# One more load buffer in the last batch, the chain to w_out's product cut into halves and parts, token logits kept in SBUF

## The chip, the cores and the metric

The kernel runs on one core of one Trainium2 chip. The metric is the time of one execution on the device in microseconds (us), as the median of several runs. Besides, one execution was profiled; it has a time and a span (first to last instruction) of its own.

## What is computed

Three layers follow each other, all in float32. Attention over 4 batches of 12 heads, 448 tokens and 64 columns gives `x` (1792 x 768), with a sigmoid in place of the softmax. Then

```
a = x @ w_a ; b = x @ w_b          # 768 -> 1536
x = (a * b) @ w_out                # 1536 -> 768
```

and last a layer of soft slots with 8 experts of 4 slots each:

```
logits = x @ phi                          # 1792 x 32
d = softmax of logits over all tokens     # per slot
slot_input = d.T @ x                      # 32 x 768
h = relu(slot_input[e] @ w1[e])           # 768 -> 1024, 8 experts
slot_out[e] = h @ w2[e]                   # 1024 -> 768
c = softmax of logits over the 32 slots   # per token
out = c @ slot_out                        # 1792 x 768
```

The experts' weights are read once: `w1` as 24 tiles of 128 x 2048 (1.05 MB each), `w2` as 32 tiles of 128 x 1536 (0.79 MB each), 50.3 MB in all.

## The kernel before, in words

The product with `w_out` is never formed for the tokens. The kernel keeps G = a * b (transposed, 12 chunks of 128 rows x 448 tokens per batch, five buffers `gT_all`), takes the logits as G times `wphi` = `w_out @ phi`, and sums d.T @ G over the batches into `acc`. Only that sum, 32 slots x 1536, is multiplied by `w_out` (line 773), which gives the slots' inputs.

A batch b of the part with w_a and w_b is the generator `ab` (line 476): 12 chunks, each of 18 matmuls for a and 18 for b (line 490), with `a` copied to `gT_all` by ACT (line 499) and multiplied by DVE (line 502). Into its gaps `fill_step` puts other work: `group` (line 445) adds four chunks to the logits `lps` (matmul line 453, add line 457) and turns them to token order (lines 467 to 469); `LG` (line 570) makes the running softmax over tokens (`logits`, line 522), turns logits and exponentials to token order (`tokens`, line 554), and adds to `acc` (`dg`, line 561). For batches 0 to 2 the logits in token order go from a tile `ltok` to a buffer `clog32` in HBM (line 579) and come back at the end (line 762). Attention of batch b + 1 runs beside batch b of `ab`. The weight halves of w_a and w_b are read for each batch again, 128 x 768 at a time (`load_w`, line 404), and split into a high and a low part by `split` (line 413: DVE or ACT, then POOL).

In the last batch, where attention is done, the room left is opened as load buffers ("slots") of 128 x 2048 for w_out (5 tiles, "wo"), w1 and w2. All of them are read in one order, `queue` (line 663). `pump` (line 669) takes the next tile of the queue and the next open slot and issues one load on SP; it is called 24 times in the last batch, and by `done` (line 698) whenever the products of a tile have freed its slot. Pool `e1` has 16 slots: 2 to 15 are open from the start of the last batch, slot 1 holds `lsd2` and slot 0 the raw weights `wr` first. `gkp` gives one slot. Pool `e2` lies in the room of the batch's x and split weights, which is free after the last a * b: its slots 1 to 4 are opened there (line 751), its slot 0 holds `gk_3` first and is opened after `last_LG` (line 758). That makes 22 slots.

`last_LG` (line 596) is the chain between the last a * b and w_out's product: logits of the last four chunks, sum over the four groups (`selF`, line 524), maximum, exponentials (line 541), exponentials to token order (line 558), `dg` (line 567) into `gp`, `acc` (line 614), its transposes (line 618), the copy to `GT` (line 619). Then come w_out's product (line 773), two steps that spread it to the experts (lines 776 to 783), w1's products (line 793, 24 tiles in groups of four), w2's (line 817) and the output.

The order on each engine is the order of the code; tiles wait for each other by semaphores which a layer below adds. SP issues its loads in order too, so a load that waits holds up those behind it.

Of the kernel before, what the change touches and what calls it, by code (L numbers as in the profile page):

```python
# [26 lines left out]
NE1, NE2 = 16, 5  # L27
# [6 lines left out]
def body(ctx, tc, q, k, v, w_a, w_b, w_out, phi, w1, w2, out):  # L34
# [55 lines left out]
    clog32 = drp.tile([T, C, B, NS], F32, name="clog32")  # L90
# [7 lines left out]
    clog = misc[:T, B * S + 256:B * S + 768].rearrange("p (c b s) -> p c b s", c=C, b=B)  # L98
# [300 lines left out]
    NCH = B * KF  # L399
    w_raw, w_sp = {}, {}  # L400
# [44 lines left out]
    def group(b, gi, evac=(act.copy, dve.tensor_copy) * 2):  # L445

        if (b, gi) != (B - 1, 2):
            for _ in range(GDEL):
                yield
# [8 lines left out]
        if (b, gi) == (B - 1, 2):  # L458
            gk = e2.tile([128, 2048], F32, tag="e20", name="gk_3")
        else:  # L460
            gk = gk_01[:, gi] if gi < 2 else gk_2
# [12 lines left out]
        gtok[b, gi] = gk  # L474

    def ab(b):
        for fc in range(KF):
# [7 lines left out]
            for i in range(2):  # L485
                wh, wl = ws[i]
                t = ps_tile("ab", [128, S], 2)
                for s, (w, xi) in enumerate(((wh, 0), (wh, 1), (wl, 0))):
# [5 lines left out]
                    if s == 2:  # L494
# [75 lines left out]
    def LG(b):  # L570
# [25 lines left out]
    def last_LG():  # L596

        run["ms"], run["lsd"] = 0, (lps, gT_all[3])
        lg, gr = logits(B - 1), group(B - 1, 2, (act.copy, dve.tensor_copy, act.copy, act.copy))
        next(gr)  # L600
        next(lg)
        next(lg)
        next(gr)
        next(lg)
        next(gr)
        dtok = stat.tile([T, C, NS], F32, tag="ltok", name="dtok", bufs=1)
        tokens(run["lsd"][1], dtok)
        for _ in gr:
            pass
        next(lg, None)  # L610
        gp = ms((128, FF // 4))
        for groups in ((0, 1), (2,)):
            dg(B - 1, dtok, gp, groups)
        dve.scalar_tensor_tensor(acc, acc, run["al"], gp, op0=ALU.mult, op1=ALU.add)
# [4 lines left out]
        act.copy(GT, gt)  # L619
        dve.tensor_scalar(rs, run["s"], 1e-9, None, op0=ALU.add)  # L620
        dve.reciprocal(out=rs, in_=rs)

# [43 lines left out]
    def open_slots(pl, names):  # L666
        slots.extend((pl, f"{pl.name}{i}") for i in names)

    def pump():

        if not queue or not slots:
            return
        what = queue.pop(0)
        pl, nm = slots.pop(0)
        t = pl.tile([128, 2048], F32, tag=nm, name=nm)
# [20 lines left out]
        ring[what] = t, pl, nm  # L696

    def done(what):
        slots.append(ring.pop(what)[1:])
        pump()  # L700
# [55 lines left out]
    run["banks"] = 2  # L756
    last_LG()
# [78 lines left out]
    for b in range(2 * B):  # L836
        pl, nm = slots.pop(0)
        o.append(pl.tile([128, 2048], F32, tag=nm, name="o")[:T, :2 * DM].rearrange(
# [37 lines left out]
```

## Time and profile before

| what | us |
|---|---|
| median of 3 runs | 737.91 |
| lowest, highest | 735.6, 739.79 |
| profiled execution, its own time | 734.16 |
| its span | 732.1 |
| PE busy in the span | 684.2 (93%) |

The 2.06 us between the profiled execution's time and its span lie around the first and last instruction. PE (TensorE) is busy most of the time, but not evenly: from some 200 us to the end of the last a * b at 609.8 us it is never idle, and after 640 us it waits for loads. The granted clock of PE is 1.00 of full speed nearly everywhere, and under it in some stretches after 660 us.

### The profile page before, as it was taken

To read this page: it belongs to the slowest core of one execution; us is meant where nothing else is said; L and a number is where in the kernel's file an instruction comes from. 1 tells how busy PE (TensorE), PEld (TensorE's weight loads), DVE (VectorE), ACT (ScalarE), POOL (GpSimd) and SP (SyncE) were. 2 spreads that over 40 slices of the span, in tenths; PEclk is the share of its full clock that TensorE was granted. 3 is DMA by queue.
4 is the path that set the end of the run, shared out by engine and by line. 5 is a ranking of instruction groups with operands and counts; after the bars stand their busy time and mean duration, and the time that the engine had idled before them with its cause. 6 is when DMAs were issued, how large, how long until landed. Compare 5 with 4: busy or idle time off the path is not lost.

```text
span 732.1 us, 10834 instructions
## 1 busy us (share of the span) xinstructions
PE 684.2 (93%) x4231; PEld 488.1 (67%) x4231; DVE 311.5 (43%) x452; ACT 271.9 (37%) x469; POOL 246.4 (34%) x151
## 2 busy tenths in 40 slices
PE   6999998999999999999999999999999998996682
PEld 4446776777777687787776887868889895441131
DVE  3567998899853323233333232313322232210012
ACT  4778778679643414233144141330201002110021
POOL 0106766666662233242431432324444542000000
PEclk9999999999999999999999999999999999999986
DMA  8858999899971432322423222310978937999958
GB/s 225 195 150 237 300 293 284 270 288 278 291 210 43 133 100 68 117 78 81 155 61 107 87 80 75 87 45 3 324 288 316 351 88 297 402 416 416 416 202 288
DMA packets 102930, 148.99 MB, mean 204 GB/s; under 512 B 51168, under 2 KB 76512, under 8 KB 99808
## 3 DMA queue, kind: packets, MB, share of 16 engines
q1 hardware_dynamic: 102880, 148.31, 61.8%
q8 instruction: 33, 0.54, 0.3%
q14 instruction: 17, 0.14, 0.1%
HBM read 128.46 MB, written 19.83 MB: 203 GB/s over the span
## 4 chain that ended last, share of the span: by engine, by line
PE 75%; DMA 13%; DVE 5%; ACT 3%; POOL 1%; issue 1%; SPq 0%; DVEq 0%; ACTq 0%; POOLq 0%
PE ab L490 44%; PE sc L191 9%; DMA e<-in_moe_w 7%; PE sc L177 7%; PE sc L793 3%; PE ms L145 3%; PE ms L467 2%; DMA wr_cv<-in_moe_w_a 2%; DVE gk L315 2%; PE ms L453 1%; PE ab L177 1%; PE ms L567 1%; DMA wr_all<-in_moe_w_b 1%; DMA out<-w 1%; DMA kn<-in_k 1%
## 5 line engine op out<-in xcount | busy, mean ns | idle before, releaser
L418 POOL TENSOR_TENSOR wl<-wr_all,wh 128x768 fp32r<-128x768 f32 x50 | 92.3, 1846 | 204.9 <-DVE wh L417 122.7
L490 PE MATMUL ab<-xh,wh 128*128 128x448 f32 x576 | 142.1, 377 | 1.4 <-ACT wh L417 1.4
L490 PE MATMUL ab<-xh,wl 128*128 128x448 f32 x576 | 141.8, 376 | 0.0
L490 PE MATMUL ab<-xl,wh 128*128 128x448 f32 x576 | 136.2, 371 | 0.0
L490 PEld LDWEIGHTS ab<-xh,wh 128*128 128x128 f32 x576 | 103.3, 188 | 20.9 <-issue 10.9
L490 PEld LDWEIGHTS ab<-xh,wl 128*128 128x128 f32 x576 | 104.1, 188 | 18.2 <-issue 8.6
L490 PEld LDWEIGHTS ab<-xl,wh 128*128 128x128 f32 x576 | 106.0, 188 | 15.4 <-issue 7.3
L181 ACT ACTIVATE a<-sc,nlog 112x448 f32<-112x448 f32 x168 | 93.5, 639 | 59.3 <-PE sc L177 59.1
L320 POOL TENSOR_TENSOR w<-gk,cy 128x768 int32<-128x768 int32 x36 | 66.2, 1838 | 99.7 <-DVE gk L315 69.5
L502 DVE TENSOR_TENSOR misc<-misc,ab 128x448 f32<-128x448 f32 x48 | 29.7, 618 | 125.8 <-PE ab L490 125.8
L499 ACT COPY misc<-ab 128x448 f32<-128x448 f32 x48 | 25.7, 536 | 153.2 <-PE ab L490 148.4
L191 PE MATMUL sc<-a,vn 112*64 112x448 f32 x384 | 76.1, 544 | 0.0
L418 POOL TENSOR_TENSOR wl<-wr,wh 128x768 fp32r<-128x768 f32 x22 | 40.5, 1839 | 53.7 <-DVE wh L417 45.7
L191 PEld LDWEIGHTS sc<-a,vn 112*64 112x64 f32 x384 | 26.0, 137 | 41.5 <-issue 38.7
L417 DVE CAST wh<-wr_all 128x768 fp32r<-128x768 f32 x50 | 35.2, 704 | 37.1 <-POOL wl L418 22.9
L817 PE MATMUL sc<-e,gk 128*32 128x384 f32 x240 | 36.4, 584 | 14.5 <-DMA e<-in_moe_w 14.2
L418 POOL TENSOR_TENSOR wl<-w,wh 128x768 fp32r<-128x768 f32 x24 | 44.9, 1869 | 3.1 <-ACT wh L417 3.1
L202 ACT ACTIVATE xh<-sc 128x448 fp32r<-128x448 f32 x24 | 13.1, 544 | 70.5 <-PE sc L191 70.5
L313 DVE TENSOR_SCALAR mf<-gk 128x768 f32<-128x768 f32 x36 | 34.1, 947 | 8.1 <-ACT gk L302 7.8
L203 DVE TENSOR_TENSOR xl<-sc,xh 128x448 fp32r<-128x448 f32 x24 | 15.0, 623 | 52.2 <-ACT xh L202 52.2
L817 PEld LDWEIGHTS sc<-e,gk 128*32 128x32 f32 x240 | 10.4, 126 | 39.7 <-DMA e<-in_moe_w 26.2
L177 PE MATMUL sc<-qh,kh 64*112 64x448 f32 x168 | 35.0, 412 | 0.6 <-ACT qh L138 0.6
(166 smaller groups left out, 764.2 us busy)
## 6 DMA issues: line engine op xcount, KB each, us to landing
e<-in_moe_w SPq DMA_DIRECT2D x23, 1024.0 KB, 7.9
e<-in_moe_w SPq DMA_DIRECT2D x27, 768.0 KB, 15.1
wr_all<-ab SPq DMA_DIRECT2D x50, 384.0 KB, 3.4
wr_cv<-in_moe_w_a SPq DMA_DIRECT2D x12, 768.0 KB, 7.2
wr_all<-in_moe_w_b SPq DMA_DIRECT2D x12, 768.0 KB, 6.7
wr_all<-in_moe_w_out SPq DMA_DIRECT2D x12, 768.0 KB, 7.2
ab<-w SPq DMA_DIRECT2D x24, 384.0 KB, 7.3
wr<-ab SPq DMA_DIRECT2D x22, 384.0 KB, 4.0
```

The costliest lines, as they stand in the source:

```text
L145: pe.transpose(t[:, c * T:(c + 1) * T], a[:, c].rearrange("p h d -> p (h d)"), ident[:T, :T])
L177: pe.matmul(sc[h], kx[r, cs], qx[r], start=(i == 0), stop=(i == 2))
L181: act.activation(a, sc[h], AF.Sigmoid, bias=nlog[:T], scale=1.0 / math.sqrt(D))
L191: pe.matmul(pv_t[g][64 * h:64 * h + 64], qkv_t["v", g][:, h, c, :], a_t.pop((g, h, c)), start=(c == 0), stop=(c == C - 1))
L313: dve.tensor_scalar(mf, m, LOW, HIGH, op0=ALU.max, op1=ALU.min)
L320: pool.tensor_tensor(thirds(w), m.bitcast(I32), thirds(cy_t.pop(x)), op=ALU.add)
L417: rnd(wh, t)
L418: pool.tensor_tensor(wl, t, wh.bitcast(F32), op=ALU.subtract)
L490: pe.matmul(t, w[:, kk * 128:(kk + 1) * 128], xt[b * NP + kk][xi], start=(s == 0 and kk == 0), stop=(s == 2 and kk == KD - 1))
L499: act.copy(gT_all[n % 5], t)
L502: dve.tensor_tensor(g, g, t, op=ALU.mult)
L817: pe.matmul(sps[h][32 * j:32 * j + 32], hT[:, 2 * x + i, 2 * j + g], ring[order2[n + j]][0][:, i, c0:c0 + w], start=(g == 0 and x == 0 and ...
```

## The change

Three things change.

- Slots. `e1` has 17 slots, of which 2 to 16 (15 instead of 14) are open from the start of the last batch; the last two are of 128 x 1536 and take only the tiles wo 3, wo 4 and w2. `e2` has 4 instead of 5. The sum is 22 as before. `pump` looks for a slot that the next tile of the queue fits in, small ones first, and does nothing if there is none; `done` calls it until it does nothing.
- Chain. The last a * b, the logits' matmul and add, the sum over groups and the maximum go by halves of 224 columns; `dg` and `acc` in two parts (groups 0 and 1, group 2); the copy to `GT` in two parts; all 16 transposes to token order stand ahead of those of the exponentials. The copy of the logits out of PSUM (`ls_3`) moves from behind the exponentials to the end.
- Token logits. `clog` is a tile in SBUF that `tokens` writes directly; three writes to HBM and one read back are gone.

```diff
-NE1, NE2 = 16, 5
+NE1, NE2 = 17, 4
...
-                            dve.tensor_tensor(g, g, t, op=ALU.mult)
+                            for cs in HALF if n == NCH - 1 else (slice(0, S),):
+                                dve.tensor_tensor(g[:, cs], g[:, cs], t[:, cs], op=ALU.mult)
...
-        ltok = stat.tile([T, C, NS], F32, tag="ltok", name="ltok", bufs=1)
-        tokens(run["lsd"][0], ltok)
-        sp.dma_start(out=clog32[:, :, b], in_=ltok)
+        tokens(run["lsd"][0], clog[:, :, b])
...
     def last_LG():
...
+        for cs in HALF:
+            for j in range(4):
+                pe.matmul(t[32 * j:32 * j + 32, cs], wphi[:, 8 + j], gT[b, 8 + j][:, cs], start=True, stop=True)
+            dve.tensor_tensor(lps[:, cs], lps[:, cs], t[:, cs], op=ALU.add)
+        lf = ms()
...
+        for cs in HALF:
+            pe.matmul(lf[:, cs], selF.rearrange("p j s -> p (j s)"), lps[:, cs], start=True, stop=True)
...
+            for i in range(4):
+                pe.transpose(tps[c][:, i * 128:(i + 1) * 128], gT[b, 8 + i][:, c * T:(c + 1) * T], ident)
...
+        dve.tensor_reduce(mx, lf[:, HALF[0]], axis=AX.X, op=ALU.max)
+        dve.tensor_tensor(m1, run["m"], mx, op=ALU.max)
+        dve.tensor_reduce(mn, lf[:, HALF[1]], axis=AX.X, op=ALU.max)
+        dve.tensor_tensor(m1, m1, mn, op=ALU.max)
...
+        act.activation(d, lf, AF.Exp, bias=nm, accum_out=sm)
...
+        tokens(d, dtok)
+        act.copy(gk[:, 2], tps[2])
+        act.copy(gk[:, 3], tps[3])
...
+        dg(b, dtok, gp, (0, 1))
+        parts = (slice(0, 256), slice(256, 384))
+        dve.scalar_tensor_tensor(acc[:, parts[0]], acc[:, parts[0]], al, gp[:, parts[0]], op0=ALU.mult, op1=ALU.add)
+        dg(b, dtok, gp, (2,))
+        dve.scalar_tensor_tensor(acc[:, parts[1]], acc[:, parts[1]], al, gp[:, parts[1]], op0=ALU.mult, op1=ALU.add)
         gt = ms((128, FF // 4))
         for gi in range(3):
             cs = slice(gi * 128, (gi + 1) * 128)
             pe.transpose(gt[:, cs], acc[:, cs], ident)
-        act.copy(GT, gt)
+        act.copy(GT[:, parts[0]], gt[:, parts[0]])
+        act.copy(GT[:, parts[1]], gt[:, parts[1]])
...
+        act.copy(ls_3, lf)
...
+            small = pl.name == "e1" and i >= NE1 - 2
+            slots.append((pl, f"{pl.name}{i}", 1536 if small else 2048))
...
+        need = 1536 if queue and (queue[0][0] == "w2" or queue[0][0] == "wo" and queue[0][1] >= 3) else 2048
+        fit = [s for s in slots if s[2] >= need]
+        if not queue or not fit:
+            return False
         what = queue.pop(0)
-        pl, nm = slots.pop(0)
-        t = pl.tile([128, 2048], F32, tag=nm, name=nm)
+        slot = min(fit, key=lambda s: s[2] > need)
...
     def done(what):
-        slots.append(ring.pop(what)[1:])
-        pump()
+        slots.append(ring.pop(what)[1])
+        while pump():
+            pass
...
-    tokens(run["lsd"][0], clog[:, :, B - 1])
+    tokens(ls_3, clog[:, :, B - 1])
     experts_consts()
-    sp.dma_start(out=clog[:, :, :B - 1], in_=clog32[:, :, :B - 1])
```

What it does to the order shows at three places. In the rows, "waits X" names the semaphore of the engine or DMA queue waited for (PE_49, DVE_49, Activation_49, Pool_49, DMAHW0_49 to DMAHW7_49), x4 counts equal instructions in a row.

First, PE at the start of the chain, behind the last matmul of line 490. Before (`wphi` logits into tile ms, `selF` sum, transposes, exponentials to token order at line 558):

```order
L453 MATMUL ms<-misc,wphi 32x448 [waits PE_49]
L453 MATMUL ms<-misc,wphi 32x448 x2
L453 MATMUL ms<-misc,wphi 32x448 [waits DVE_49]
L524 MATMUL ms<-misc,selF 128x448 [waits DVE_49]
L467 MATMUL sc<-ident,misc 112x128 x8
L558 MATMUL sc<-ident,misc 112x32 [waits Activation_49]
L558 MATMUL sc<-ident,misc 112x32 x3
L467 MATMUL sc<-ident,misc 112x128 [waits PE_49]
```

Now (the lines are those of the changed kernel; 599 answers to 453, 606 to 524, 612 to 467, 555 to 558):

```order
L599 MATMUL ms<-misc,wphi 32x224 [waits PE_49]
L599 MATMUL ms<-misc,wphi 32x224 x2
L599 MATMUL ms<-misc,wphi 32x224 [waits DVE_49] x2
L599 MATMUL ms<-misc,wphi 32x224 x3
L606 MATMUL ms<-misc,selF 128x224 [waits PE_49]
L606 MATMUL ms<-misc,selF 128x224 [waits DVE_49]
L612 MATMUL sc<-ident,misc 112x128 x12
L612 MATMUL sc<-ident,misc 112x128 [waits PE_49]
L612 MATMUL sc<-ident,misc 112x128 x3
L555 MATMUL ab<-ident,misc 112x32 [waits Activation_49]
```

Two of the eight wphi matmuls wait for DVE: the fourth of the first half, for the first half of a * b, and the first of the second half; by its count that one waits for DVE's add of the first half. All 16 transposes now stand ahead of line 555.

Second, PE at the end of the chain, from the transposes of `acc` to w_out's product. Before (line 558 here turns the logits of the last batch to token order):

```order
L618 MATMUL ms<-ident,acc 128x128 [waits DVE_49]
L618 MATMUL ms<-ident,acc 128x128 x2
L558 MATMUL ms<-ident,misc 112x32 x4
L773 MATMUL sc<-e_4989,misc 32x512 [waits DMAHW7_49,Activation_49]
L773 MATMUL sc<-e_4989,misc 32x512 x3
```

Now (638 answers to 618, 806 to 773):

```order
L564 MATMUL ab<-gk_5777,dtok 32x128 [waits DVE_49]
L564 MATMUL ab<-gk_5777,dtok 32x128 x7
L638 MATMUL ms<-ident,acc 128x128 [waits PE_49]
L638 MATMUL ms<-ident,acc 128x128
L638 MATMUL ms<-ident,acc 128x128 [waits DVE_49]
L555 MATMUL ms<-ident,misc 112x32 [waits PE_49,Activation_49]
L555 MATMUL ms<-ident,misc 112x32 x3
L806 MATMUL sc<-e_4985,misc 32x512 [waits DMAHW5_49]
L806 MATMUL sc<-e_4985,misc 32x512 x3
```

The second part of `dg` (line 564 on gk_3) waits for DVE, which before it did not: by its count, for the add of the first part to `acc`. Line 555 waits for ACT, by its count for the copy of the logits at line 643, which stands behind both copies to `GT` on ACT; w_out's product stands behind it.

Third, SP's loads from the last a * b on. Before:

```order
L695 DMA e21_5752<-in_moe2_w1 128x2048 [waits PE_49]
L695 DMA e22_5754<-in_moe2_w1 128x2048 [waits DMAHW6_49]
L695 DMA e23_5756<-in_moe2_w1 128x2048
L695 DMA e24_5758<-in_moe2_w1 128x2048
L695 DMA e20_5856<-in_moe2_w1 128x2048 [waits DVE_49,PE_49,Activation_49]
L762 DMA misc_97<-clog32_104 112x4x96 [waits PE_49]
L695 DMA e12_5884<-in_moe2_w1 128x2048 [waits PE_49]
L695 DMA e13_5890<-in_moe2_w1 128x2048 [waits DMAHW4_49,PE_49]
L695 DMA e14_5896<-in_moe2_w1 128x2048 [waits DMAHW5_49,PE_49]
L695 DMA e15_5904<-in_moe2_w1 128x2048 [waits DMAHW6_49,PE_49]
L695 DMA e16_5912<-in_moe2_w1 128x2048 [waits DMAHW7_49,PE_49]
L695 DMA e17_5946<-in_moe2_w1 128x2048 [waits DMAHW0_49,PE_49]
```

Now:

```order
L726 DMA e21_5749<-in_moe2_w1 128x2048 [waits DMAHW3_49,PE_49]
L726 DMA e22_5751<-in_moe2_w1 128x2048
L726 DMA e23_5753<-in_moe2_w1 128x2048 [waits DMAHW5_49]
L726 DMA e20_5862<-in_moe2_w1 128x2048 [waits DVE_49,PE_49,Activation_49]
L726 DMA e12_5889<-in_moe2_w1 128x2048 [waits PE_49]
L726 DMA e13_5895<-in_moe2_w1 128x2048 [waits PE_49]
L726 DMA e14_5901<-in_moe2_w1 128x2048 [waits PE_49]
L726 DMA e15_5947<-in_moe2_w1 128x2048 [waits DMAHW2_49,PE_49]
...
L726 DMA e18_5953<-in_moe2_w1 128x2048 [waits DMAHW5_49,PE_49]
L726 DMA e115_5955<-in_moe2_w2 128x1536 [waits DMAHW6_49]
L726 DMA e116_5957<-in_moe2_w2 128x1536 [waits DMAHW7_49]
```

Before, w_out's product released five loads (e12 to e16) and w1's first group the next ones (from e17). Now it releases three (e12 to e14); e15 to e18 wait for w1's first group, and the two small slots e115 and e116, which w_out's product frees too, take the first tiles of w2 only behind them (the rows of e16 and e17, like that of e15, are left out).

## Rows read from the trace of the kernel before

**Rows 1.** The page, slices: what the DMA engines moved in 40 equal slices of 18.3 us.

```profile
GB/s 225 195 150 237 300 293 284 270 288 278 291 210 43 133 100 68 117 78 81 155 61 107 87 80 75 87 45 3 324 288 316 351 88 297 402 416 416 416 202 288
```

**Rows 2.** The chain that ended last, from 560 us on: start, length, what.

```profile
611.60 0.63 DVE misc L457
...
612.28 1.02 PE ms L524 x2
...
616.57 2.78 PE ab L567 x64
...
619.38 0.61 DVE acc L614
...
620.63 0.49 ACT misc L619
...
621.16 4.08 PE sc L773 x48
...
629.11 10.44 PE sc L793 x96
...
652.88 15.06 DMA e<-in_moe_w
...
706.07 1.48 PE sc L817 x10
```

**Rows 3.** SP's timeline in short windows from 605 us on: start, length, loads issued.

```profile
605.60 0.33 SPq L695 DMA_DIRECT2D e<-in_moe_w  x1
...
609.87 2.06 SPq L695 DMA_DIRECT2D e<-in_moe_w  x4
...
619.40 0.33 SPq L695 DMA_DIRECT2D e<-in_moe_w  x1
...
622.29 0.34 SPq L695 DMA_DIRECT2D e<-in_moe_w  x1
...
632.69 1.28 SPq L695 DMA_DIRECT2D e<-in_moe_w  x3
```

**Rows 4.** Line 695, window 605 to 606: the load issued at 605.60, issue to landing.

```profile
DMA to landing us min/median/max: 4.9/4.9/4.9
```

**Rows 5.** Windows: length, busy times (count), PE clock, DMA share, GB/s last.

```profile
540.00:580.00 40.00, 40.00 (x210) 35.58 (x212) 11.04 (x17) 4.28 (x8) 17.59 (x10) 1.00 0.90 332
...
609.90:612.00 2.10, 1.66 (x8) 0.16 (x5) 1.02 (x2) 0.00 (x0) 0.00 (x0) 1.00 0.51 105
...
621.00:628.00 7.00, 6.15 (x57) 3.48 (x57) 1.04 (x2) 1.17 (x3) 0.00 (x0) 1.00 0.99 345
628.00:640.00 12.00, 12.00 (x105) 4.22 (x104) 3.78 (x7) 1.22 (x2) 0.00 (x0) 1.00 1.02 419
633.20:707.00 73.80, 58.26 (x431) 19.75 (x424) 2.08 (x3) 2.30 (x5) 0.00 (x0) 0.91 0.98 398
```

**Rows 6.** Timeline of 605 to 632 us: start, length, engine, instruction.

```profile
609.95 0.62 DVE L502 TENSOR_TENSOR misc<-misc,ab 128x448 f32<-128x448 f32 x1 [6.35 <-PE ab L490]
...
613.13 1.04 PE L467 MATMUL sc<-ident,misc 128*112 128x128 f32 x8
...
613.34 0.62 DVE L527 TENSOR_REDUCE mx<-ms 128x1 f32<-128x448 f32 x1 [1.11 <-PE ms L524]
...
613.99 0.16 DVE L531 TENSOR_TENSOR mn<-mn,mx 128x1 f32<-128x1 f32 x1
...
614.38 0.63 ACT L541 ACTIVATE misc<-ms,nm 128x448 f32<-128x448 f32 x1
...
615.59 0.29 DVE L559 COPY dtok<-sc 112x128 f32<-112x128 f32 x1 [0.58 <-PE sc L558]
```

**Rows 7.** Groups by form on PE, 605 to 640 us: count, busy us, mean ns, idle before.

```profile
L567 PE MATMUL ab<-gk,dtok 112*32 112x256 f32 x32 | 1.9, 382 | 0.0
...
L567 PE MATMUL ab<-gk,dtok 112*32 112x128 f32 x32 | 1.1, 273 | 0.0
```

**Rows 8.** Groups by form on ACT, 600 to 732 us: count, busy us, mean ns.

```profile
L469 ACT COPY gk<-sc 112x512 f32<-112x512 f32 x2 | 1.2, 585 | 7.7 <-PE sc L467 7.7
```

More of the change, by code (lines that the diff above doesn't have):

```diff
@@ L89, in body @@
     out32 = drp.tile([128, KF, DM], F32, name="out32")
-    clog32 = drp.tile([T, C, B, NS], F32, name="clog32")
     idj = ident.rearrange("p (j s) -> p j s", j=4)
@@ L97, in body @@
     SI = small[:, 1536:2304]
-    clog = misc[:T, B * S + 256:B * S + 768].rearrange("p (c b s) -> p c b s", c=C, b=B)
+    clog = const.tile([T, C, B, NS], F32, name="clog")
     selE = small[:, 2304:2560].rearrange("p (j g m) -> p j g m", j=4, g=2)
@@ L399, in body @@
     NCH = B * KF
+    HALF = (slice(0, S // 2), slice(S // 2, S))
     w_raw, w_sp = {}, {}
@@ L445, in group @@
     def group(b, gi, evac=(act.copy, dve.tensor_copy) * 2):
-        if (b, gi) != (B - 1, 2):
-            for _ in range(GDEL):
-                yield
+        for _ in range(GDEL):
+            yield
         t = ms()
@@ L457, in group @@
             dve.tensor_tensor(lps, lps, t, op=ALU.add)
[L458 to L461, printed above, removed]
+        gk = gk_01[:, gi] if gi < 2 else gk_2
         gk = gk[:T].rearrange("p (c n) -> p c n", c=C)
@@ L596, in last_LG @@
     def last_LG():
[L598 to L610, printed above, removed]
-        gp = ms((128, FF // 4))
-        for groups in ((0, 1), (2,)):
-            dg(B - 1, dtok, gp, groups)
@@ L614, in last_LG @@
-        dve.scalar_tensor_tensor(acc, acc, run["al"], gp, op0=ALU.mult, op1=ALU.add)
+        b = B - 1
+        run["ms"] = 0
+        d = gT_all[3]
+        t = ms()
+        for cs in HALF:
[3 more added lines that the diff above has]
+        lf = ms()
+        mx, nm, mn, dm, sm, al, sn = (stat.tile([128, 1], F32, tag=x, name=x)
+                                      for x in ("mx", "nm", "mn", "dm", "sm", "al", "sn"))
@@ new lines, in last_LG @@
+        m1 = stat.tile([128, 1], F32, tag="m1", name="m1")
+        for cs in HALF:
+            pe.matmul(lf[:, cs], selF.rearrange("p j s -> p (j s)"), lps[:, cs], start=True, stop=True)
+        gk = e2.tile([128, 2048], F32, tag="e20", name="gk_3")[:T].rearrange("p (c n) -> p c n", c=C)
+        tps = []
+        for c in range(C):
+            tps.append(ms((T, 512)))
+            for i in range(4):
+                pe.transpose(tps[c][:, i * 128:(i + 1) * 128], gT[b, 8 + i][:, c * T:(c + 1) * T], ident)
@@ new lines, in last_LG @@
+        gtok[b, 2] = gk
+        dve.tensor_reduce(mx, lf[:, HALF[0]], axis=AX.X, op=ALU.max)
+        dve.tensor_tensor(m1, run["m"], mx, op=ALU.max)
+        dve.tensor_reduce(mn, lf[:, HALF[1]], axis=AX.X, op=ALU.max)
+        dve.tensor_tensor(m1, m1, mn, op=ALU.max)
+        dve.tensor_scalar(nm, m1, -1.0, None, op0=ALU.mult)
+        dve.tensor_tensor(dm, run["m"], m1, op=ALU.subtract)
+        act.copy(gk[:, 0], tps[0])
+        act.activation(d, lf, AF.Exp, bias=nm, accum_out=sm)
+        act.activation(al, dm, AF.Exp)
@@ new lines, in last_LG @@
+        dve.tensor_copy(gk[:, 1], tps[1])
+        dtok = stat.tile([T, C, NS], F32, tag="dtok", name="dtok", bufs=1)
+        tokens(d, dtok)
+        act.copy(gk[:, 2], tps[2])
+        act.copy(gk[:, 3], tps[3])
+        dve.scalar_tensor_tensor(sn, run["s"], al, sm, op0=ALU.mult, op1=ALU.add)
+        gp = ms((128, FF // 4))
+        dg(b, dtok, gp, (0, 1))
+        parts = (slice(0, 256), slice(256, 384))
+        dve.scalar_tensor_tensor(acc[:, parts[0]], acc[:, parts[0]], al, gp[:, parts[0]], op0=ALU.mult, op1=ALU.add)
@@ L618, in last_LG @@
             pe.transpose(gt[:, cs], acc[:, cs], ident)
-        act.copy(GT, gt)
-        dve.tensor_scalar(rs, run["s"], 1e-9, None, op0=ALU.add)
+        act.copy(GT[:, parts[0]], gt[:, parts[0]])
+        act.copy(GT[:, parts[1]], gt[:, parts[1]])
+        dve.tensor_scalar(rs, sn, 1e-9, None, op0=ALU.add)
         dve.reciprocal(out=rs, in_=rs)
+        act.copy(ls_3, lf)
     def combine_weights():
@@ L666, in open_slots, with slot_tile @@
     def open_slots(pl, names):
-        slots.extend((pl, f"{pl.name}{i}") for i in names)
+        for i in names:
+            small = pl.name == "e1" and i >= NE1 - 2
+            slots.append((pl, f"{pl.name}{i}", 1536 if small else 2048))
+    def slot_tile(s, name=None):
+        pl, nm, n = s
+        return pl.tile([128, n], F32, tag=nm, name=name or nm)
     def pump():
-        if not queue or not slots:
-            return
+        need = 1536 if queue and (queue[0][0] == "w2" or queue[0][0] == "wo" and queue[0][1] >= 3) else 2048
+        fit = [s for s in slots if s[2] >= need]
+        if not queue or not fit:
+            return False
         what = queue.pop(0)
-        pl, nm = slots.pop(0)
-        t = pl.tile([128, 2048], F32, tag=nm, name=nm)
+        slot = min(fit, key=lambda s: s[2] > need)
+        slots.remove(slot)
+        t = slot_tile(slot)
         if what[0] == "wo":
@@ L756, in body @@
     run["banks"] = 2
+    ls_3 = lps
     last_LG()
@@ L836, in body @@
     for b in range(2 * B):
-        pl, nm = slots.pop(0)
-        o.append(pl.tile([128, 2048], F32, tag=nm, name="o")[:T, :2 * DM].rearrange(
+        o.append(slot_tile(slots.pop(0), "o")[:T, :2 * DM].rearrange(
             "p (c n) -> p c n", c=2))
```

3 lines of the change are left out of this document (2 added, 1 removed).

## The prediction, made before the changed kernel was run

> **What bounds the kernel now.** I read the slices first, then the chain of waits for the end, SP's issues in that stretch, and last the load rate in windows. PE is never idle from 540 to 580 us [rows 5], and so up to the last a * b. The loads are idle at two places and full at the end: the rate falls to 88 GB/s in the slice 586 to 604 us and is 402 to 416 GB/s from 622 to 695 us [rows 1]. So the slots are full before the batch ends, and everything behind it is paced by loads. The chain says the same: from 652.88 us on its long pieces are loads, until PE's last w2 products at 706.07 us [rows 2]. From there to the end of the span (26 us) the change touches nothing. The end therefore moves by as much as the last load of w2 moves, and that depends on two things: how many bytes are still to be moved when the slots open, and whether SP has a load to issue at all times.
>
> **Bytes.** By the last a * b, 17 loads are issued before (5 of w_out, 12 of w1); the 17th goes at 605.60 us, four more at 609.87, one at 619.40 when `dg` has used gk_3, then five from 622.29 on as w_out's product frees its slots, and the next at 632.69 behind w1's first group [rows 3]. With the change 18 are issued by the last a * b, then three, one, three, and nothing until w1's first group: the two small slots fit w2 only, and the queue's head is w1. The 18th falls into the idle stretch, where it costs nothing. One load less is 1,049 KB, the read back of the logits another 172 KB; at 419 GB/s [rows 5] these are 2.9 us. The rate is 345 GB/s from 621 to 628 us against 419 behind [rows 5], while the 384-byte pieces of that read are under way; were all of this dip the read's, its going would give 7 x (419 - 345) = 518 KB, 1.2 us in all with its own bytes, so that the whole gain is at most some 3.7 us. That counts only while the loads never run dry.
>
> **The chain to w_out's product**, before from 609.95 us to 621.16 us. By DVE's 0.62 us for 448 columns and 0.16 for one [rows 6], 224 columns cost 0.39.
> - To the maximum's start. Before: product 0.62, logits 1.03 (end of 502 to 611.60), add 0.63, sum 1.11 (612.23 to 613.34) [rows 2, 6]. Now: 0.39; then the halves' matmuls. w1's matmuls, four side by side and two instructions each, take 10.44 x 8 / 96 = 0.87 us for 512 columns [rows 2], so 448 columns stream for 0.76 and half of them save 0.38: 0.65; add 0.39; the second half's logits only then, 0.65 and 0.15 for its four weight loads (my estimate); add 0.39; sum 0.73. That is 3.35 against 3.39: nothing won, since the second half waits for the first half's add.
> - Maximum to exponentials: 613.34 to 614.38, 1.04 us [rows 6]. The two halves of the reduction both wait for the whole sum, by the order of the matmuls and of DVE: one more start of 0.16 and one more small step, 1.30 in all, +0.26.
> - Exponentials to `dg`: before, dtok is ready at 615.88 [rows 6], but eight transposes stand ahead of `dg`, which starts at 616.57 [rows 2]. Now all 16 stand ahead of the exponentials' transposes, and at 1.04 us for eight [rows 6] they are through by then: -0.65.
> - `dg` to the transposes' end: 616.57 to 620.63 before [rows 2]. Now 1.9 us [rows 7], 0.05, the first add to acc 0.48 (0.61 less 128 columns at 1.05 ns), 0.05, 1.1 [rows 7], 0.05, the second add 0.34, one transpose 0.37 (estimate, of the 0.64 for three): 4.34, +0.28, as the second part waits for the first add.
> - Copy to w_out: 620.63 to 621.16, 0.53 [rows 2]. Now ACT copies 256 and 128 columns and then 448 of the logits, at 0.59 for 512 [rows 8] and 0.49 for 384 [rows 2] some 0.37, 0.28 and 0.53 less 0.16 of overlap; PE's transposes of the logits wait for the third and w_out stands behind them, 0.3 more: 1.35, +0.8.
>
> Sum: -0.04 + 0.26 - 0.65 + 0.28 + 0.8 = +0.65; w_out starts at 621.8 instead of 621.16.
>
> That the second half waits is in the order shown above; no row of the trace before has DVE at a PSUM tile that PE is writing. The Trainium skill ("PSUM — Partial Sum Buffer", section "PSUM bank collisions raise a hardware error") says that two engines must not touch one bank and quadrant at once, disjoint columns included, so software has to keep them apart. By that rule the sum stands; without it the first rival's would.
>
> **The queue.** The four tiles of w1's first group come free together, 632.69 - 621.16 = 11.53 us after w_out starts [rows 2, 3]. From an issue into an idle queue to the full rate it takes 1.6 us: 609.87 to 612.00 brought 105 GB/s x 2.1 us = 220 KB, as much as 0.5 us at full rate [rows 3, 5]. As upper end I take the lone load's 4.9 us to landing [rows 4] less 2.5 of transfer, 2.4. So the loads flow again at 621.8 + 11.53 + 1.6 = 634.95 us. What is left then is 4 of w1 and 32 of w2, 29.36 MB. Before, just that much was left at 633.2 us: 398 GB/s x 73.8 us = 29.37 MB [rows 5]. So the change ends **1.7 us later**. The other way round: with the change the queue is empty from 618.9 to 621.3 (three loads instead of four), from 623.8 to 624.5, and from 632 to 634.95 us, 6 us; against the gain of 3.7 that is some +2, which agrees. With 2.4 for the restart it is +2.5.
>
> The Trainium skill ("SBUF — State Buffer", section "The DMA setup-cost knee (why "@ 1 MiB" ≠ asymptote)") gives about 2 us as the fixed part of every transfer. With it for the 1.6 the sum would be +2.1, the same case; the lone load's 4.9 us are above its 2 + 1,049 KB / 436 GB/s = 4.4.
>
> What else moves costs nothing: the three writes of token logits leave SP's queue in stretches where PE is never idle; `tokens` writes the same 128 columns (0.29 us [rows 6]). DVE's reduction over 16 x 32 logits no longer waits for a load; PE is busy with w1 then.
>
> **The forecast** is 734.16 + 1.7 = 735.9 us against the profiled execution. The median of the runs is 737.91, 3.75 above that execution, so 739.6 us on its scale: +0.24%, which a measurement of this kernel can't tell from no change (it can tell some 0.5%, 3.7 us).
>
> **Rivals.**
> - *The halves overlap after all*, the add of one beside the matmul of the other. Then the exponentials start 1.3 us earlier than in my sum, but wait for the 16 transposes (2.1 us); `dg` starts at 615.1, runs in one piece of 2.8, and w_out starts at 619.7 even with the logits' copy ahead: 619.7 + 13.13 - 633.2 = -0.4, 737.5 us. Against it: the waits in the order. Chance 0.12.
> - *The loads never run dry*, because SP issues w1's rest earlier. Then the full 3.7 us come in: 734.2 us. It decides by e15's issue: it would have to come by 630.4 us, and it waits for w1's first group at 633.3. Chance 0.05.
> - *The extra load delays the weight halves of a and b*, which share its queue between 582 and 605 us. If one half lands later than PE needs it, PE stops for up to one load's 2.5 us, and w_out starts that much later: +4.2, 742.1 us, slower by 0.57%. For it: the load stands ahead of a weight half on SP. Against it: at 332 GB/s from 540 to 580 us, such pairs ran one after the other and PE was busy 40.00 of 40 us [rows 5]. It decides once a weight half is late by more than its lead over PE, which no row shows. Chance 0.11.
>
> My forecast has 0.72. Faster by over 0.5%: the second rival's 0.05 and a little scatter, 0.06. Slower by over 0.5%: most of the third rival, and the upper end of my sum with scatter, 0.13. Within: 0.81. The range runs from 736.5 (between the first two rivals) to 742.2 us (the third).
>
> **What would show it.** Right: the loads' rate near 0 for 2 to 3 us around 619 to 621 and again around 632 to 635; w_out's first product at 621.5 to 622; SP issuing three loads, then none for some 9 us; `dg` with a gap of 0.5 us between its parts; the last w2 products 1 to 3 us later than 706. Wrong: a load rate above 400 throughout 612 to 640, or w_out at 620 or earlier, or PE idle before 609.8 us.

## The result, and the profile after

| | before | with the change |
|---|---|---|
| median, us (20 runs each) | 736.32 | 739.34 |
| lowest, highest | 731.69, 740.16 | 736.67, 747.49 |
| profiled execution, its own time | 734.16 | 740.74 |
| its span | 732.1 | 738.7 |
| ratio of the times | 1 | 1.0054, interval 1.0032 to 1.0075 |

The change costs 0.54%, some 4.0 us (by the 95% interval 2.4 to 5.5). The medians lie 3.0 us apart and the means 3.9 (736.3 and 740.2), as a few executions of the changed kernel are long. The forecast was 739.6 us and +1.7 us. The sign came out, and the time lies in the range, but the change cost about twice what the sum says (1.8 times by the medians, 2.4 times by the ratio). The likeliest case, "no change that can be told", is just missed by the ratio: its bound is 0.5%, "slower by over 0.5%" had a chance of 0.13, and the interval reaches to both sides of that bound.

Two profiled executions can't be subtracted as they stand. The last a * b begins at 609.95 us before and at 612.78 after, though the two programs do nearly the same up to there (the changed one issues one load more and writes no token logits to HBM). So I count everything **from the start of DVE's last a * b product on** ("behind the last a * b"), and took three profiles of the kernel before and four of the changed one. How that reads in the changed kernel's own profile: first the chain, in the timeline of DVE and PE (start, length, engine, instruction, then the idle time before it and what ended it).

```profile
612.78 0.69 DVE L499 TENSOR_TENSOR misc<-misc,ab 128x224 f32<-128x224 f32 x2 [6.35 <-PE ab L486]
...
614.27 0.59 PE L599 MATMUL ms<-misc,wphi 128*32 128x224 f32 x8 [0.48 <-DVE misc L600]
...
618.14 0.40 PE L555 MATMUL ab<-ident,misc 32*112 32x32 f32 x4 [0.37 <-ACT misc L621]
...
618.92 1.93 PE L564 MATMUL ab<-gk,dtok 112*32 112x256 f32 x32 [0.38 <-DVE dtok L556]
621.46 1.08 PE L564 MATMUL ab<-gk,dtok 112*32 112x128 f32 x32 [0.60 <-DVE acc L632]
...
624.41 0.41 PE L555 MATMUL ms<-ident,misc 32*112 32x32 f32 x4 [1.07 <-ACT misc L643]
624.74 5.76 PE L806 MATMUL sc<-e,misc 128*32 128x512 f32 x48
```

Three waits are new, in the places that the forecast names: the second half's matmuls wait 0.48 us for DVE's add of the first half, the second part of `dg` 0.60 us for the first add to `acc`, and the logits' transposes 1.07 us for ACT's copy (line 643). w_out's product starts 12.03 us behind the last a * b; before it was 11.21 [rows 2, 6]. One thing was not expected: w_out's product takes 5.76 us instead of 4.08 [rows 2]. (The chain below and the table further down give 5.69 for it and a start of 624.81: they leave out its first 0.07 us, beside the last transposes.) The windows over it (length, busy times, PE's granted clock, DMA share, GB/s last) say why:

```profile
622.00:624.00 2.00, 1.24 (x23) 0.61 (x15) 0.57 (x3) 0.62 (x3) 0.66 (x1) 1.00 0.40 61
624.00:626.00 2.00, 1.59 (x12) 0.69 (x16) 0.29 (x1) 0.35 (x1) 0.00 (x0) 0.69 0.81 311
626.00:628.00 2.00, 2.00 (x12) 0.39 (x8) 0.00 (x0) 0.00 (x0) 0.00 (x0) 0.50 0.76 217
628.00:630.00 2.00, 2.00 (x32) 0.84 (x28) 0.72 (x1) 0.00 (x0) 0.00 (x0) 0.96 0.78 291
```

The granted clock is 1.00 up to 624 us, falls while w_out's product begins, stands at 0.50 (1.2 instead of 2.4 GHz), and is back at some 629 us. The loads' rate is down to 61 GB/s at 622 to 624 us, since SP waits and issues one load in these 2 us. SP's own rows (start, length, loads) and its longest waits show the second empty stretch; the last line is that of the kernel before:

```profile
622.64 0.33 SPq L726 DMA_DIRECT2D e<-in_moe_w  x1
...
626.74 2.87 SPq L726 DMA_DIRECT2D e<-in_moe_w  x3
...
637.96 2.17 SPq L726 DMA_DIRECT2D e<-in_moe_w  x4
```

```profile
SPq L726 <- PE sc L826: 8.8, 3, 8.4
SPq L726 <- PE ab L564: 8.6, 1, 8.6
SPq L726 <- PE sc L806: 5.6, 3, 3.8
```

```profile
SPq L695 <- PE sc L793: 7.5, 3, 6.6
```

By [rows 3] SP before issued one load at 619.40 us, others from 622.29 on as w_out's product went, and the next at 632.69. Now it is one, three, and nothing until 637.96: one wait of 8.4 us for w1's first group. Before, that wait was 6.6 us, with five loads under way instead of three, and the rate did not fall [rows 5]. The chain that ended last goes through w_out's product and the products of w1's first two groups, for which SP waits (the second group ends at 641.51), and then through loads alone:

```profile
624.81 5.69 PE sc L806 x48
...
634.38 7.13 PE sc L826 x64
641.51 0.22 SPq L726
...
641.82 17.68 DMA e<-in_moe_w
...
704.95 7.82 DMA gkp<-in_moe_w
```

PE's last w2 products follow at 712.82 us, 100.04 behind the last a * b; before, 706.07 - 609.95 = 96.12 [rows 2, 6].

The slices say the same from farther off; against [rows 1] the 34th slice (where the chain and w_out's product are) falls from 297 to 290 and the 35th from 402 to 319 GB/s, while the full rate of 416 behind them is the same:

```profile
GB/s 214 186 152 213 296 285 289 285 277 291 290 212 46 129 99 67 119 73 98 137 68 112 67 99 55 87 44 35 321 282 331 354 87 290 319 414 416 416 201 290
```

### The profile page after: what moved, and what is told of

The parts are those of the page before. It is cut to its first block, busy times and chain, and to the rows that moved or that the text cites. A ratio compares the mean times of both kernels' runs of the same rounds, so it can differ in the third digit from the quotient of the medians.

```text
span 738.7 us, 10846 instructions
## 1 busy us (share of the span) xinstructions
PE 690.8 (94%) x4241; PEld 490.7 (66%) x4241; DVE 308.0 (42%) x457; ACT 272.3 (37%) x470; POOL 247.4 (33%) x151
## 5 line engine op out<-in xcount | busy, mean ns | idle before, releaser
L499 DVE TENSOR_TENSOR misc<-misc,ab 128x448 f32<-128x448 f32 (+1 forms) x49 | 29.7, 609 | 128.1 <-PE ab L486 128.1
L190 PEld LDWEIGHTS sc<-a,vn 112*64 112x64 f32 x384 | 26.3, 139 | 42.6 <-issue 40.0
L850 PEld LDWEIGHTS sc<-e,gk 128*32 128x32 f32 x240 | 9.9, 123 | 38.0 <-DMA e<-in_moe_w 26.3
```

The costliest lines, as they stand in the source:

```text
L190: pe.matmul(pv_t[g][64 * h:64 * h + 64], qkv_t["v", g][:, h, c, :], a_t.pop((g, h, c)), start=(c == 0), stop=(c == C - 1))
L499: dve.tensor_tensor(g[:, cs], g[:, cs], t[:, cs], op=ALU.mult)
L850: pe.matmul(sps[h][32 * j:32 * j + 32], hT[:, 2 * x + i, 2 * j + g], ring[order2[n + j]][0][:, i, c0:c0 + w], start=(g == 0 and x == 0 and ...
```

## The experiments

Twelve runs were made: seven other kernels, the changed kernel three more times and the kernel before twice. The ratio is always to runs of the kernel before beside them on the same chip, with its 95% interval. The times in the last four columns are from the run's one profile; the starts and ends are us behind the last a * b.

| kernel | ratio | w_out's product starts | w_out's product, us | last w2 products | end of span |
|---|---|---|---|---|---|
| before | 1 | 11.21 | 4.08 | 96.12 | 122.15 |
| before, second, third profile | | 11.22, 11.22 | 4.08, 4.08 | 96.36, 96.38 | 122.64, 122.10 |
| changed | 1.0054 (1.0032 to 1.0075) | 12.03 | 5.69 | 100.04 | 125.92 |
| changed, second profile | 1.0057 (1.0035 to 1.0080) | 12.02 | 4.01 | 98.14 | 124.37 |
| changed, third, fourth profile | | 12.03, 12.03 | 5.64, 5.70 | 100.00, 100.04 | 125.97, 125.92 |
| logits' copy early | 1.0048 (1.0027 to 1.0069) | 11.02 | 4.08 | 97.23 | 123.45 |
| chain alone | 1.0033 (1.0009 to 1.0058) | 12.02 | 4.01 | 98.27 | 124.27 |
| slots and token logits, no chain | 1.0016 (0.9992 to 1.0039) | 11.21 | 4.08 | 97.27 | 122.98 |
| PE kept busy in the pauses | 1.0047 (1.0023 to 1.0071) | 12.02 | 4.01 | 98.00 | 123.56 |
| out of turn, copy early | 0.9992 (0.9967 to 1.0017) | 11.02 | 4.08 | 95.94 | 121.92 |
| out of turn, no chain | 0.9982 (0.9962 to 1.0003) | 11.21 | 4.08 | 94.34 | 120.33 |
| out of turn, whole columns | 0.9997 (0.9974 to 1.0020) | 10.65 | 4.08 | 94.43 | 120.18 |

**The logits' copy early.** The chain's last term, tried alone:

```diff
         act.activation(al, dm, AF.Exp)
+        act.copy(ls_3, lf)
         dve.tensor_copy(gk[:, 1], tps[1])
...
         dve.tensor_scalar(rs, sn, 1e-9, None, op0=ALU.add)
-        act.copy(ls_3, lf)
```

Expected:

> The changed kernel with one line moved: the copy of the logits out of PSUM stands behind the exponentials on ACT again, not behind the copies to GT. All stretches are measured from the start of DVE's last a * b product: w_out's product starts 11.21 us behind it before and 12.03 us with the change, the span ends 122.15 and 125.92 us behind it. Theory: three parts make up the 3.8 us, the logits' copy ahead of w_out (0.8), PE's clock at half in w_out's product because PE had too little to do ahead of it (1.6), and loads that run dry since the small slots take no w1 (the rest). Then w_out starts at 11.2 and the end comes 0.8 us earlier at least, 125.1; if the shorter pause also keeps the clock up, 2.4 us earlier, 123.5. Rival (the slots alone decide, the loads are dry whatever the chain does): the end stays at 125.9. Against the kernel before: ratio 1.001 to 1.004 by the theory, 1.005 by the rival.

w_out's product starts 11.02 us behind the last a * b, 1.01 us before the changed kernel and before the kernel before as well. So the 0.8 us that the forecast put on the copy is right in kind and a little short, and without it the rest of the chain is 0.2 us faster than the old one. Its last w2 products stand at 97.23, still 0.9 behind the three profiles of before (mean 96.29). The timed ratio moved less than that: 1.0048, inside the interval of the changed kernel, above the 1.001 to 1.004 of the theory and next to the rival's 1.005. The profile bears the theory out (the end at 123.45, 2.5 us earlier); the timing can't tell the two apart, as its interval holds both and the plain means of the same runs give 1.0034.

**The chain alone, with the slots of before.**

```diff
-NE1, NE2 = 17, 4
+NE1, NE2 = 16, 5
...
-            small = pl.name == "e1" and i >= NE1 - 2
+            small = False
```

The token logits go through HBM again here, as SBUF has no room for them when all slots are full ones.

> The chain's part of the change alone: slots as before (16 and 5, all of 2048) and token logits through HBM as before. Theory: w_out starts at about 12.0 us behind the last a * b and its product takes 5.7 us at half clock, but w_out frees five loads instead of three, whose transfer covers the wait for w1's first group (3.7 us of cover in the kernel before), so the end comes at 122 to 123.7 us, within 1.5 us of the kernel before. Rival (the chain alone costs it all): 125.9 us. Ratio 1.000 to 1.002 against 1.005.

w_out's product starts at 12.02, as in the changed kernel: the chain's delay of 0.8 us is whole and belongs to the chain. Its product ran at the full clock, where I expected the half one. The loads never run dry (the rate is 295 GB/s or more in every 2 us from 614 to 646), yet the ratio, 1.0033, and the end, 124.27, lie between the two expectations. Its last w2 products stand 2.0 us later than before. 0.65 us of that are load: 364 GB/s in the first 24.5 us behind the last a * b against 375. Where the rest goes I didn't find. With the 1.0 us of the next kernel the two parts alone cost more than the 1.85 us of both together at the full clock, so parts read from one profile each can't be added to a tenth.

**The slots and the token logits, with the chain of before.** The functions of the chain (`last_LG`, `group`) are those of before; the slots and `clog` are the changed kernel's.

```diff
-                            for cs in HALF if n == NCH - 1 else (slice(0, S),):
+                            for cs in (slice(0, S),):
...
-        for cs in HALF:
-            pe.matmul(lf[:, cs], selF.rearrange("p j s -> p (j s)"), lps[:, cs], start=True, stop=True)
...
+        lg, gr = logits(B - 1), group(B - 1, 2, (act.copy, dve.tensor_copy, act.copy, act.copy))
```

> The other two parts alone: the changed kernel's slots and token logits in SBUF, with the chain of the kernel before (whole columns, one piece of dg, the logits' copy behind the exponentials). Theory: w_out starts at 11.2 us at full clock, three loads follow it and then none until w1's first group, so the loads stand still for some 3 us and the end comes 1.1 us later than before, at 123.2 us (122.7 to 124). Rival (the slots are a gain, only the chain loses): the end comes 1 to 3 us earlier than before, at 119 to 121. Ratio 1.0015 against under 0.999.

1.0016 (0.9992 to 1.0039), as the theory says, and the rival's gain is excluded: the slots that are meant to load more cost time, or at best nothing. w_out's product starts at 11.21 to the hundredth as before, and still the last w2 products come 1.0 us later. In its trace the rate is 25 GB/s at 632 to 634 us, and SP's wait for w1 is as long as in the changed kernel:

```profile
SPq L703 <- PE sc L802: 9.4, 4, 8.4
```

The bytes say why. Windows of 24.5 us from the last a * b on, GB/s last; before, then this kernel, then the changed kernel's second profile:

```profile
609.95:634.45 24.50, 21.14 (x213) 10.95 (x211) 8.93 (x21) 5.59 (x12) 2.81 (x13) 1.00 0.96 375
```

```profile
610.62:635.12 24.50, 21.14 (x213) 10.95 (x211) 8.93 (x21) 5.59 (x12) 2.80 (x13) 1.00 0.82 307
```

```profile
613.63:638.13 24.50, 20.76 (x215) 11.11 (x213) 9.59 (x26) 5.62 (x13) 2.81 (x13) 1.00 0.81 303
```

Before, 24.5 x 375 = 9.19 MB are moved there; with the new slots 7.52 MB. The new slots had 1.05 MB less to do there (the 18th load) and no read back of 0.17 MB, so they would have been level at 7.97. They are 0.45 MB short, 1.1 us at 416 GB/s, and 97.27 - 96.29 = 1.0 us is what the end moved. The gain in bytes is there; the empty queue takes more than it.

**PE kept busy in the pauses.** Three matmuls more, whose product nobody reads, of 160, 96 and 320 columns in three of PE's pauses, so this kernel does a little work more than the changed one:

```diff
+        warm = ps_tile("sc", [128, 512], 4)
+        pe.matmul(warm[:, :160], ident, wphi_f[:, :160], start=True, stop=True)
...
+        pe.matmul(warm[:, :96], ident, wphi_f[:, :96], start=True, stop=True)
...
+        pe.matmul(warm[:, :320], ident, wphi_f[:, :320], start=True, stop=True)
```

> The changed kernel with three matmuls added whose result nobody uses, in three of PE's pauses ahead of w_out: 160 columns between the two parts of dg, 96 behind them, 320 behind the transposes of acc. Theory (PE's clock falls because PE is too little busy from the exponentials to w_out): the clock stays at 1.00 in w_out's product, which takes 4.1 instead of 5.7 us, and the end comes 1.6 us earlier, at 124.3. Rival (the clock falls for another reason, or by chance in the one execution seen): 0.5 in w_out's first half again, the end at 125.9 or a little later. Ratio 1.003 against 1.005 or 1.006.

In its profile w_out's product takes 4.01 us at clock 1.00. But the ratio is 1.0047, and its interval holds both expectations. The next profile of the changed kernel itself also had 4.01 us, so this run alone shows nothing.

**The changed kernel again.**

> The changed kernel itself once more. Theory (slots and logits' copy, +1.7 to +1.9 us, and in some executions 1.6 us more where w_out's product runs at the half clock): ratio 1.002 to 1.005; if the half clock in w_out's product belonged to that one execution, this profile has the product at 4.1 us at clock 1.00, and the last w2 products some 98.0 us behind the last a * b. Rival (the half clock belongs to the pauses of the new chain): the product again takes 5 us or more at a clock under 0.8, and the last w2 products come 99.5 us or more behind the last a * b.

The time is the same again, 1.0057; in this execution the clock stays at 1.00. Here the change can be read without the half clock: the chain is equal to a hundredth (12.02), SP issues one, three, and then the next at 637.11,

```profile
623.48 0.33 SPq L726 DMA_DIRECT2D e<-in_moe_w  x1
...
626.71 2.19 SPq L726 DMA_DIRECT2D e<-in_moe_w  x3
...
637.11 2.60 SPq L726 DMA_DIRECT2D e<-in_moe_w  x5
```

and the rates of 2 us around the empty stretches are

```profile
622.00:624.00 2.00, 1.60 (x35) 1.15 (x35) 0.76 (x4) 0.00 (x0) 1.50 (x7) 1.00 0.30 127
624.00:626.00 2.00, 0.93 (x9) 0.45 (x12) 0.35 (x2) 0.98 (x3) 0.00 (x0) 1.00 0.76 193
...
636.00:638.00 2.00, 2.00 (x24) 0.65 (x20) 1.06 (x3) 0.00 (x0) 0.00 (x0) 1.00 0.03 12
638.00:640.00 2.00, 2.00 (x24) 0.60 (x20) 0.00 (x0) 0.00 (x0) 0.00 (x0) 1.00 0.98 258
```

The last w2 products come 98.14 - 96.29 = 1.85 us later than before. The forecast had 1.7.

**Small slots out of turn.** If the empty queue is what costs, then the two small slots, open while the queue's head is a tile of w1 that doesn't fit, are the cure: let them take the next tile of w2. Three kernels have this:

```diff
-        if not queue or not fit:
+        if not queue or not slots:
             return False
-        what = queue.pop(0)
+        at = 0
+        if not any(s[2] == 2048 for s in slots):
+            at = next((n for n, q in enumerate(queue) if q[0] == "w2" or q[0] == "wo" and q[1] >= 3), None)
+            if at is None:
+                return False
...
+        what = queue.pop(at)
```

With the chain by halves and the logits' copy early:

> The changed kernel, but a small slot that is open while no large one is takes the next tile of w2 out of turn, and the logits' copy stands behind the exponentials. Theory (the dry stretch behind w_out is what the small slots cost): loads go on at 632 to 635 us, the last w2 products come 94.5 to 95.5 us behind the last a * b instead of 97.2 (with the copy alone moved); the time is 2 to 3 us below that of the early copy, ratio 0.9985 to 1.002. Rival (the end is set by the half clock, not by loads): the time stays at 1.0045 to 1.005.

With the chain of before:

> The slots and the token logits of the change with the chain of before, and small slots filled out of turn. Theory: the run without it stood at 1.0016 with one dry stretch of some 2.5 us behind w_out; that goes, so 0.9975 to 0.9990, the last w2 products 94.5 to 95.5 us behind the last a * b (before 96.1). Rival (the dry stretch is covered by what PE has in stock): 1.001 to 1.002.

With the chain in whole columns, all 16 transposes ahead, `dg` in one piece and the copy early:

> As the last, and the chain in whole columns with all 16 transposes ahead of the exponentials, dg in one piece and the logits' copy behind the exponentials. Theory: w_out starts some 10.5 us behind the last a * b (before 11.2, with the change 12.0), and with the loads never dry behind w_out the ratio is 0.9965 to 0.9985, 0.5 to 1 us faster than the run with the chain of before. Rival (PE's pauses in any chain of this form lower its clock in some executions): 1.000 to 1.002, slower than the run with the chain of before, and the granted clock under 1.00 in w_out's product.

In the kernel with the chain of before SP now issues five loads instead of three while w_out's product runs, the rate behind it stays full, and in 24.5 us it moves 8.65 MB, above the break-even of 7.97:

```profile
628.10 3.40 SPq L708 DMA_DIRECT2D e<-in_moe_w  x5
```

```profile
SPq L708 <- PE sc L807: 8.8, 2, 7.1
```

```profile
615.77:640.27 24.50, 21.14 (x213) 10.95 (x211) 8.92 (x21) 5.60 (x12) 2.81 (x13) 1.00 0.90 353
634.00:638.00 4.00, 4.00 (x36) 1.68 (x39) 3.17 (x7) 1.22 (x2) 0.00 (x0) 1.00 0.99 418
638.00:640.00 2.00, 2.00 (x24) 0.54 (x19) 0.53 (x1) 0.00 (x0) 0.00 (x0) 1.00 1.03 418
```

SP still waits 7.1 us for w1's first group; with five loads under way the rate holds. Its last w2 products come at 94.34, 2.9 us ahead of the same kernel without the rule (97.27) and 1.9 ahead of before. This is what the slots bring when the queue stays full, 1.9 of the 3.7 us that the forecast named as the most. With the early copy the rule gives 1.3 (97.23 to 95.94), less than expected; in whole columns the end stands at 94.43. The times follow: 0.9992, 0.9982 and 0.9997. All three intervals lie below that of the changed kernel, and each holds 1: against the kernel before no gain is shown by the times. For the second one the profile has 1.9 us, and the times give 1.3 (-0.2 to 2.8). The kernel in whole columns came between its two expectations, with w_out's product at clock 1.00; its w_out starts 0.56 us earlier than before and gives the end nothing over the chain of before. Against the same kernel with the chain by halves and parts (11.02) whole columns start w_out 0.37 us earlier, so the splitting itself cost time here.

**Second and third profiles.** The open question was why the measured 4.0 us exceed the 1.85 of the profile with the full clock.

> The kernel before, for a second profile. Measured so far: the changed kernel +4.0 us; of these its traces show 2.2 us behind the last a * b, and 1.6 more in the execution with the half clock in w_out's product. Theory (the rest is that half clock, in some executions): the last a * b at 612 to 614 us here too, since the half clock in the first 200 us strikes every version, and from it 122.0 to 122.7 us to the end. Rival 1 (the rest lies ahead of the last a * b): the last a * b again at 610.0, where the changed kernel had it at 612.8 and 613.6. Rival 2 (the end of the kernel before varies as much): more than 123 us from it to the end.

> The changed kernel, for a third profile. Theory: w_out's product either 4.1 us at clock 1.00 and 124.4 us from the last a * b to the end, or 5 us and more at the half clock and 125.5 to 126; the last a * b at 610 to 616. Rival 1 (the rest lies ahead): the last a * b at 612.5 to 614 again, and 124.4 to the end.

> The kernel before, for a third profile. Theory: the last a * b somewhere from 610 to 614, w_out's product 4.1 us at clock 1.00, 122.0 to 122.7 us from the last a * b to the end. Rival 1: the last a * b at 610.0. Rival 2: more than 123 us to the end, or w_out's product at the half clock.

> The changed kernel, for a fourth profile. Theory: as for the third: 124.4 us to the end with w_out's product at clock 1.00, or 125.5 to 126 with it at the half clock. Rival 1: the last a * b at 612.5 to 614 again, and 124.4 to the end.

The kernel before had its last a * b at 612.66 and 611.90 us here, so the 609.95 of its first profile was a good execution; over all versions it stands at 609.95 to 616.14. In both, w_out's product took 4.08 us and the end came 122.64 and 122.10 us behind it, so the second rival falls. The first one is not settled: the last a * b averages 611.50 us in the three profiles of before and 613.76 in the four of the changed kernel, and these positions scatter by more than that. With the clock at 1.00 in the first 200 us both programs have it at the same place: the kernel with the early copy, which up to there is the changed one, at 609.95 as well. The changed kernel had the half clock in its third and fourth profile too: in three of four. In the fourth one the windows of 1 us show where it falls, and the timeline what stood there:

```profile
624.00:625.00 1.00, 0.79 (x8) 0.45 (x12) 0.29 (x1) 0.15 (x1) 0.00 (x0) 0.92 0.69 254
625.00:626.00 1.00, 1.00 (x9) 0.23 (x5) 0.00 (x0) 0.00 (x0) 0.00 (x0) 0.50 1.06 451
626.00:627.00 1.00, 1.00 (x12) 0.36 (x8) 0.00 (x0) 0.00 (x0) 0.00 (x0) 0.50 0.49 205
627.00:628.00 1.00, 1.00 (x12) 0.28 (x8) 0.00 (x0) 0.00 (x0) 0.00 (x0) 0.50 0.92 131
628.00:629.00 1.00, 1.00 (x12) 0.26 (x8) 0.00 (x0) 0.00 (x0) 0.00 (x0) 0.87 0.82 328
```

```profile
624.21 0.40 PE L555 MATMUL ms<-ident,misc 32*112 32x32 f32 x4 [1.07 <-ACT misc L643]
624.54 5.77 PE L806 MATMUL sc<-e,misc 128*32 128x512 f32 x48
```

Where the half clock is there, the end comes another 100.03 - 98.14 = 1.9 us later. Averages over the profiles: last w2 products at 99.56 with the change (four) and 96.29 before (three), 3.3 us. That leaves 0.7 of the 4.0 measured, well inside the interval; it may lie ahead of the last a * b.

## Why the prediction was right, and where it fell short

- **What bounds the kernel.** Right. The end moves with the last load of w2: from the last w2 products to the end of the span it is 25.5 to 26.3 us in every kernel.
- **The chain.** Right in its order, and nearly so term by term. Forecast 0.65 us later at w_out, measured 0.81 (12.02 against 11.21); the last two terms, from `dg` to the copy to `GT` (618.92 to 623.38 us) and from there to w_out (624.81), are +0.40 and +0.90 instead of +0.28 and +0.8. The exponentials were put at 614.60 us on the scale of before and came at 617.36 - 2.83 = 614.53; `dg` at 616.1 and came at 618.92 - 2.83 = 616.09; the copy of the logits at +0.8 and its undoing gave 1.01. Next to nothing (0.1 us) was won by halves up to the maximum, as the second half waits for the first half's add (the 0.48 us above), so the rival of overlapping halves falls. The Trainium skill ("PSUM — Partial Sum Buffer", section "PSUM bank collisions raise a hardware error") has software keep two engines out of one bank and quadrant; that the wait is there agrees with it.
- **The queue.** Right with the clock at 1.00. Empty stretches were forecast at 618.9 to 621.3 and 632 to 634.95 us on the scale of before; in the second profile, 3.68 us later on its own scale, the low rates lie at 622 to 626 and 636 to 640. The restart was put at 1.6 us: loads issued at 637.11 bring 258 x 2 = 516 KB until 640, so the full rate begins 1.66 us behind the issue. The Trainium skill ("SBUF — State Buffer", section "The DMA setup-cost knee (why "@ 1 MiB" ≠ asymptote)") has about 2 us as the fixed part of one transfer up to its completion; the restart of the queue, which is not quite the same thing, took less in this row. Forecast for the end 1.7 us, measured 1.85 at that clock.
- **The step that fell short** is "The four tiles of w1's first group come free together, 632.69 - 621.16 = 11.53 us after w_out starts". That took the durations of w_out's product and of what follows from rows at the full clock. With the change it holds in one profile of four (637.11 - 625.65 = 11.46); in the other three it is 13.10 to 13.16 (in the first 637.96 - 624.81 = 13.15), since w_out's product runs at the half clock. So the term was mis-sized by 1.6 us in such executions, and their end comes 1.9 us later, some 1.4 on the average of the four. Their last w2 products are 3.7 us later than before, outside the 1 to 3 us that the prediction gave as a sign. I priced PE's new pauses as time on the chain and nothing else. In the 8.03 us ahead of w_out's product PE is busy 6.08 us before and 5.50 with the change:

```profile
613.13:621.16 8.03, 6.08 (x92) 4.38 (x90) 2.99 (x11) 3.32 (x8) 2.81 (x13) 1.00 1.01 426
```

```profile
616.78:624.81 8.03, 5.50 (x88) 3.48 (x90) 2.61 (x11) 3.13 (x9) 2.82 (x13) 1.00 0.78 294
```

- **Luck.** That 739.34 us is within 0.3 us of the forecast's 739.6 is luck. The forecast stood on 737.91 us, the median of three runs; twenty runs give 736.32, 1.6 us less, and the change was put 1.3 us too low on that scale. The two errors cancel.
- **The rivals.** The loads ran dry, so the second is out. PE was busy without a break from 540 to 611 us in all four profiles of the changed kernel, so the extra load made PE wait for no weight half and the third is out as well. The rise over the forecast did not come from it.
- **What stays open.** How often the half clock strikes is known from four profiles only. That it comes from the pauses is likely, not shown: it came in three of four profiles of the changed kernel and in none of three before, none of the four kernels that fill or shorten the pause before w_out (one profile each), but also not in the one profile of the chain alone, which has the same pauses. And in those kernels with the early copy or the extra matmuls the times (1.0048, 1.0047) are some 2 us above what their profiles give (+1.2 and +1.3 us at the span's end against the mean of before, 122.30), which lies just under their intervals (from 2.0 and 1.7 us on). Slow stretches that the one profile missed are not borne out: the granted clock as a mean over whole executions, on record for every timed run, is 0.983 in the 17 runs of these two kernels and 0.983 in 63 of the kernel before. In 30 of the changed kernel it is 0.980. One half clock in w_out's product (1.7 us lost of 738, by the fourth profile) is worth 0.002 of that, so the lower mean fits it, but it doesn't say where in the execution the clock was low.

## What to carry to other kernels

A buffer more helps only if the queue's next tile fits it: here two smaller slots stood open while SP waited 8.4 us with a tile of w1 at its head, and taking the next tile that fits brought the end forward by 2.9 us in one kernel and 1.3 in another. Splitting a chain in two gained next to nothing here, where both halves go through one tile that one engine writes and another reads; and a copy that nobody needs soon, put last on the engine whose result the next product waits for, cost 1.0 us of the chain. When a change adds pauses to PE on the path, look for the granted clock behind them in several profiles: one profile of the changed kernel would have shown 1.9 or 3.7 us, by chance.

## What the runs showed of the hardware

The granted clock of TensorE fell from 1.00 to 0.50 with no pause longer than 1.07 us before it: ahead of w_out's product PE stood still for 0.48, 0.37, 0.38, 0.60 and 1.07 us between its matmuls, and the clock was at its half while w_out's product kept PE busy throughout (rows of the first profile, above). The same instructions at the same distances, in the second profile, kept the full clock. So whether it falls is not set by the program alone. The Trainium skill ("TensorE: Matmul & The Clock Gate", section "What's actually happening") ties the clock to how busy the engine has been of late and lists an idle stretch as what lowers it; in these rows PE was partly busy all along, and the clock fell in three profiles of four.

In the first 200 us the granted clock falls as well, in most executions and whatever the version, and shifts all that follows: the last a * b came at 609.95 to 610.62 us where the granted clock was 1.00 throughout (three profiles), and at 611.9 to 616.1 us where its mean over 10 us fell to 0.66 to 0.88 in one or two places (the other eleven). That is larger than the change itself, and the reason to count from the last a * b on.
